# Order of TensorE's work in a fused attention and mixing kernel: low parts last, the first turn inside an angle product, value products at the end of a half unit

## The chip, the cores and the metric

The kernel runs on one core of a Trainium2 chip. The metric is device time in microseconds (us): the median of three runs before the change is 1183.68 (1183.5 to 1184.48). The engines are named as the profile names them: PE is TensorE (its weight loads are PEld), DVE is VectorE, ACT is ScalarE, POOL is GpSimd, SP issues most DMAs.

## The reference

Eight batches of eight heads, 576 positions, head width 64. Attention keeps only scores within `tau` of a row's maximum; its output, with the heads side by side (512 wide), goes through a mixing block with sines and cosines of an angle.

```python
scores = scale * np.matmul(q, k.transpose(0, 1, 3, 2))
thresh = np.max(scores, axis=-1, keepdims=True) - tau
scores = np.where(scores >= thresh, scores, -1000000000.0)
attn = np.exp(scores - max); attn = attn / (sum + 1e-09)
x = np.matmul(attn, v)                       # heads side by side
theta = x @ w_theta
zr = x * np.cos(theta); zi = x * np.sin(theta)
y = w_tok_r @ zr + w_tok_i @ zi              # over positions, per batch
u = x + y
out = u + np.maximum(u @ w_ch, 0.0)
```

The two lines with `max` and `sum` are shortened; everything else is as the reference has it.

## The kernel before, in words

Everything on PE is in an order written out by the program; the other engines' orders come from a scheduler that goes by priorities and by a timeline of its own. PE's order is the order in which the code issues its instructions.

**Attention.** The outer loop goes over *half units* t: for each of 32 pairs of heads nine of them (four blocks of 128 queries for each of two heads, and one for the 64 queries left of both). A half unit issues, in this order: the scores of half unit t+3 (`begin`, L264, tile s_ps, one such tile in all), a piece of mixing work (`fill`), the turning round of half unit t's weights (`flip` and `flip_last`, L312 and L327, tiles t_ps), what is due at t (`todo`), and a second piece of mixing work (`fill`). Due are: the value products (`values`, L347, tile o_ps, 20 matmuls in fp32, 256 or 320 columns), the scaling of a pair's result (`normalize`, L363 to L372), at the end of a batch the splitting of its result into parts (`split_x`), and one half unit later the start of the batch's mixing.

DVE reads a score tile and frees it (L268), ACT takes the exponential (L285), DVE applies the threshold (L286), ACT copies turned weights out (L317, L319, L330, L334) and value products (L348).

**Mixing** (`moe`) is a generator that hands out its PE work in pieces with a price; each `fill` takes pieces for about 820 units of price. For exactness every factor is split into a high and a low part of reduced precision (fp32r), so that a product is three terms: high by high and two mixed ones. The four blocks of 128 columns are numbered 0 to 3; `ORDER` lists the steps:

- a0 to a3: the angles (`angle`, `product`, L381, tile th_ps): 24 matmuls each, 12 for each half h of the positions. ACT moves them out (L416); DVE reduces them to one turn (L420, L421).
- s01 and s23: sines and cosines of two blocks (`sines`): DVE takes the magnitude (L430), ACT loads the table with sine (L434), computes two cosines and two sines (L438, L439) and loads the table with the exponential again (L443); POOL multiplies by x (L450; DVE in the last batch). ACT's group has a priority far above the rest.
- f0 to f3: turning round of z (`flip`, L462, tile z_ps), whose results ACT and DVE split into zh and zl (L464, L465). "t0f1" means: f1 in three pieces between the pieces of t0.
- t0 to t3: the products over positions (`token`, L478 to L480, tile y_ps): 27 matmuls for each half; DVE adds them to x (L482), then u is split (`split_u`, L104, L100, L109).
- last the channel products (L381, tile c_ps), again 24 matmuls for each block, and the output (L523, L527).

All PSUM tiles but s_ps share six buffers of one tag (`ps_t`). The z tiles have three buffers. The tiles in which q and k are loaded share four buffers (`temp`) with the angles.

Low parts: xl comes from POOL for blocks 0 and 1 and from DVE for 2 and 3; zl from DVE; ul from POOL for blocks 0 to 2, and from DVE for block 3, whose uh comes from ACT.

Of the kernel before, what the change touches and what calls it, by code (L numbers as in the profile page):

```python
# [10 lines left out]
F32 = mybir.dt.float32  # L11
# [20 lines left out]
ATTENTION, SINES = 20, 10000  # L32
# [3 lines left out]
ORDER = "a0 a1 s01 a2 a3 f0 s23 t0f1 t1f2 t2f3 t3"  # L36
# [3 lines left out]
def tile_attn_moe(  # L40
# [11 lines left out]
    nc = tc.nc  # L52
    B, NP, D, _, S = qT.shape
    P = 128
    DM = 512
    NM = DM // P
    HS = S // 2
    SP = S + 64
    NK = 9
# [315 lines left out]
    def product(ps, wm, parts, hs, outer=False):  # L375

        terms = [(a, bb, c) for a, bb in ((0, 0), (0, 1), (1, 0)) for c in range(NM)]
        if outer:
            terms.sort(key=lambda x: x[2])
        for n, (a, bb, c) in enumerate(terms):  # L380
            nc.tensor.matmul(ps[:, :HS], wm[:, a, c, :], parts[c][bb][:, hs], start=(n == 0), stop=(n == 11))  # L381
            if n % 4 == 3 and n < 11:
                yield 524
# [6 lines left out]
    parts = {}  # L390
# [8 lines left out]
    def moe(b):  # L399
        last = b == B - 1  # L400
# [7 lines left out]
        def angle(m):  # L408
            th = temp("th")
            wm = get_wm(0, m)  # L410
            for h in range(2):
                hs = slice(h * HS, (h + 1) * HS)
                ps = ps_t.tile([P, 512], F32, tag="t", name="th_ps")
                yield from product(ps, wm, xs, hs, outer=(m == 0 and h == 0))

                nc.scalar.activation(out=th[:, hs], in_=ps[:, :HS], func=AF.Copy, scale=1.0 / TURN)  # L416
                yield 524
# [52 lines left out]
        def token(m):  # L470
            zz = zs.pop((m, "T"))
            x = xT[b * NP + m]
            for h in range(2):
                hs = slice(h * HS, (h + 1) * HS)
                ps = ps_t.tile([P, 512], F32, tag="t", name="y_ps")
                for c in range(NK):
                    zh, zl = zz[c]
                    nc.tensor.matmul(ps[:, :HS], zh, wt_h[:, c, hs], start=(c == 0), stop=False)  # L478
                    nc.tensor.matmul(ps[:, :HS], zh, wt_l[:, c, hs], start=False, stop=False)  # L479
                    nc.tensor.matmul(ps[:, :HS], zl, wt_h[:, c, hs], start=False, stop=(c == NK - 1))  # L480
                    yield 393
# [11 lines left out]
        for what in ORDER.split():  # L493
# [3 lines left out]
            if what == "a":  # L497
                yield from angle(m)
# [17 lines left out]
        for m in range(NM):  # L516
            wm = get_wm(1, m)
            u = xT[b * NP + m]
            for h in range(2):
                hs = slice(h * HS, (h + 1) * HS)  # L520
                ps = ps_t.tile([P, 512], F32, tag="t", name="c_ps")
                yield from product(ps, wm, us, hs, outer=last or (m == 0 and h == 0))
# [3 lines left out]
                yield 524  # L526
# [45 lines left out]
    with tc.manual_schedule(engines={nc.tensor.engine}):  # L572
# [3 lines left out]
        for t, (n, i, j) in enumerate(halfs):  # L576
# [5 lines left out]
            with tc.high_priority(offset=ATTENTION):  # L582
# [5 lines left out]
                for fn, a in todo.pop(t, ()):  # L588
                    fn(*a)
# [7 lines left out]
            fill()  # L597
            if n + 1 < B * NP:
# [60 lines left out]
```

## Time and profile before

| what | value |
|---|---|
| median of three runs | 1183.68 us |
| profiled execution | 1179.78 us, span 1178.0 us |
| PE busy | 1049.4 us (89%) |
| DVE, ACT, POOL busy | 853.2, 748.9, 381.9 us |
| mean granted PE clock | 0.956 of full speed |

The profiled execution is 3.9 us below the median of the three runs; 1.8 us of it lie outside the span. Busy PE is time in which a matmul is under way, and matmuls overlap, so the waits of PE and the stretches in which its granted clock is below one say more than its busy share.

### The profile page before, as it was taken

To read this page: it belongs to the slowest core of one execution; us is meant where nothing else is said; L and a number is where in the kernel's file an instruction comes from. 1 tells how busy PE (TensorE), PEld (TensorE's weight loads), DVE (VectorE), ACT (ScalarE), POOL (GpSimd) and SP (SyncE) were. 2 spreads that over 40 slices of the span, in tenths; PEclk is the share of its full clock that TensorE was granted. 3 is DMA by queue.
4 is the path that set the end of the run, shared out by engine and by line. 5 is a ranking of instruction groups with operands and counts; after the bars stand their busy time and mean duration, and the time that the engine had idled before them with its cause. 6 is when DMAs were issued, how large, how long until landed. Compare 5 with 4: busy or idle time off the path is not lost.

```text
span 1178.0 us, 20979 instructions
## 1 busy us (share of the span) xinstructions
PE 1049.4 (89%) x7648; PEld 923.3 (78%) x7648; DVE 853.2 (72%) x2111; ACT 748.9 (64%) x1411; POOL 381.9 (32%) x295
## 2 busy tenths in 40 slices
PE   3756688999979999899989998899989999799998
PEld 2544577899869888798878987798878988699798
DVE  7999987676767767776777667776776767677462
ACT  5656677765686666865686657765687656765350
POOL 2011323531353233432344324522335313531110
PEclk9776799999989999999999999999989999899999
DMA  8623523213331152212432142311532143300421
GB/s 259 185 90 90 159 57 103 57 49 107 103 102 55 32 162 77 78 51 62 140 104 72 32 134 83 99 51 54 148 95 65 46 116 103 88 21 1 117 68 58
DMA packets 55175, 105.24 MB, mean 89 GB/s; under 512 B 11936, under 2 KB 20128, under 8 KB 55072
## 3 DMA queue, kind: packets, MB, share of 16 engines
q1 hardware_dynamic: 45856, 70.35, 20.4%
q0 software_dynamic: 9216, 33.56, 9.8%
q8 instruction: 60, 0.98, 0.3%
q14 instruction: 43, 0.35, 0.1%
HBM read 90.24 MB, written 13.63 MB: 88 GB/s over the span
## 4 chain that ended last, share of the span: by engine, by line
PE 66%; DVE 13%; ACT 9%; DMA 4%; issue 3%; POOL 2%; SPq 1%; ACTq 0%; POOLq 0%; DVEq 0%
PE o_ps L347 12%; PE s_ps L264 11%; PE t_ps L312 8%; PE y_ps L478 6%; PE y_ps L480 6%; PE c_ps L381 6%; PE y_ps L479 6%; PE th_ps L381 6%; DMA qraw<-in_qT_dram 4%; DVE sc L268 3%; DVE s_sb L286 3%; PE z_ps L462 2%; POOL xl L109 2%; ACT s_sb L285 1%; ACT z L438 1%
## 5 line engine op out<-in xcount | busy, mean ns | idle before, releaser
L268 DVE TENSOR_SCALAR_CACHE_REDUCE sc<-s_ps 128x576 f32<-128x576 f32 x288 | 217.5, 755 | 129.3 <-PE s_ps L264 125.3
L286 DVE SCALAR_TENSOR_TENSOR s_sb<-sc,nm,s_sb 128x576 f32<-128x576 f32 x288 | 258.3, 901 | 55.6 <-ACT s_sb L285 53.0
L285 ACT ACTIVATE s_sb<-sc,nm 128x576 f32<-128x576 f32 x288 | 223.4, 778 | 114.3 <-DVE sc L268 113.6
L264 PE MATMUL s_ps<-k,qq 128*128 128x288 f32 (+1 forms) x1344 | 240.0, 308 | 59.4 <-DVE sc L268 48.8
L264 PEld LDWEIGHTS s_ps<-k,qq 128*128 128x128 f32 x1344 | 202.8, 199 | 72.5 <-DVE sc L268 45.7
L347 PE MATMUL o_ps<-a,v 128*64 128x320 f32 (+1 forms) x1280 | 183.7, 433 | 20.0 <-ACT a L319 19.2
L478 PE MATMUL y_ps<-wt_h,zh 128*128 128x288 f32 x576 | 188.5, 327 | 6.7 <-DVE xT L482 5.9
L312 PE MATMUL t_ps<-ident,s_sb 128*128 128x128 f32 x1152 | 185.2, 286 | 6.3 <-ACT xT L348 4.9
L480 PE MATMUL y_ps<-wt_h,zl 128*128 128x288 f32 x576 | 172.0, 299 | 11.3 <-DVE zl L465 11.3
L479 PE MATMUL y_ps<-wt_l,zh 128*128 128x288 f32 x576 | 170.9, 297 | 0.0
L317 ACT COPY a<-t_ps 128x512 f32<-128x512 f32 x256 | 148.1, 578 | 32.1 <-PE t_ps L312 31.5
L347 PEld LDWEIGHTS o_ps<-a,v 128*64 128x64 f32 x1280 | 91.6, 144 | 91.5 <-ACT a L319 22.4
L312 PEld LDWEIGHTS t_ps<-ident,s_sb 128*128 128x128 f32 x1152 | 148.7, 147 | 9.3 <-ACT xT L348 5.8
L109 POOL TENSOR_TENSOR k<-kraw,k 128x576 fp32r<-128x576 f32 x62 | 91.9, 1483 | 197.2 <-ACT k L100 196.5
L214 POOL TENSOR_TENSOR qq<-qraw,qq 64x576 fp32r<-64x576 f32 x62 | 98.5, 1589 | 124.9 <-ACT qq L212 86.7
L178 POOL DMA_DIRECT2D wm<-wm_dram x64 | 37.0, 579 | 279.0 <-PE c_ps L381 170.9
L478 PEld LDWEIGHTS y_ps<-wt_h,zh 128*128 128x128 f32 x576 | 109.8, 191 | 14.0 <-DVE xT L482 7.5
L480 PEld LDWEIGHTS y_ps<-wt_h,zl 128*128 128x128 f32 x576 | 109.3, 190 | 13.3 <-DVE zl L465 13.3
L479 PEld LDWEIGHTS y_ps<-wt_l,zh 128*128 128x128 f32 x576 | 110.2, 191 | 0.0
L450 POOL TENSOR_TENSOR z<-z,xT 128x576 f32<-128x576 f32 x56 | 83.8, 1516 | 46.3 <-issue 32.3
L381 PE MATMUL c_ps<-uh,wm 128*128 128x288 f32 x512 | 97.6, 303 | 0.1
L381 PE MATMUL th_ps<-xh,wm 128*128 128x288 f32 x512 | 89.0, 300 | 0.4 <-ACT xh L100 0.4
(77 smaller groups left out, 1547.2 us busy)
## 6 DMA issues: line engine op xcount, KB each, us to landing
wm<-wm_dram POOLq DMA_DIRECT2D x64, 512.0 KB, 4.2
qraw<-in_qT_dram SPq DMA_DIRECT2D x128, 144.0 KB, 3.0
kraw<-in_kT_dram SPq DMA_DIRECT2D x128, 144.0 KB, 2.9
out_dram<-xT SPq DMA_DIRECT2D x32, 288.0 KB, 4.1
v<-in_vp_dram SPq DMA_DIRECT2D x32, 256.0 KB, 2.8
wraw<-in_w_tok_dram SPq DMA_DIRECT2D x9, 576.0 KB, 4.0
wraw<-in_w_theta_dram SPq DMA_DIRECT2D x4, 512.0 KB, 5.0
wm_dram<-whi SPq DMA_DIRECT2D x8, 256.0 KB, 2.3
```

The costliest lines, as they stand in the source:

```text
L109: eng_lo.tensor_tensor(out=lo, in0=src, in1=hi.bitcast(F32), op=ALU.subtract)
L264: nc.tensor.matmul(ps[:, h, d0:d1], st, kk, start=(x == 0), stop=(x == len(todo) - 1))
L268: nc.vector.tensor_scalar(out=sc.rearrange("p (a b) -> p a b", a=2), in0=ps[:, :, :HS], scalar1=-1.0, scalar2=None, op0=ALU.mult, op1=ALU.min,
L285: nc.scalar.activation(out=e, in_=u.ps[j], func=AF.Exp, bias=nm[:, j : j + 1], scale=-1.0)
L286: nc.vector.scalar_tensor_tensor(out=e, in0=u.ps[j], scalar=nm[:, 2 + j : 3 + j], in1=e, op0=ALU.is_le, op1=ALU.mult, accum_out=u.pr.rows[ ...
L312: nc.tensor.transpose(out=tp[:, c * P : (c + 1) * P], in_=u.sf[:, k0 + c * P : k0 + (c + 1) * P], identity=ident)
L317: nc.scalar.copy(out=t.a[:, :, j, q0 : q0 + P], in_=tp.rearrange("p (c q) -> p c q", c=4))
L347: nc.tensor.matmul(o[64 * j : 64 * j + 64, :w], st, mv, start=(c == 0), stop=(c == 4))
L381: nc.tensor.matmul(ps[:, :HS], wm[:, a, c, :], parts[c][bb][:, hs], start=(n == 0), stop=(n == 11))
L478: nc.tensor.matmul(ps[:, :HS], zh, wt_h[:, c, hs], start=(c == 0), stop=False)
L479: nc.tensor.matmul(ps[:, :HS], zh, wt_l[:, c, hs], start=False, stop=False)
L480: nc.tensor.matmul(ps[:, :HS], zl, wt_h[:, c, hs], start=False, stop=(c == NK - 1))
```

## The change

Three things are reordered on PE, and with them the pools' and the scheduler's choices on the other engines.

1. `product` runs high by high, then low weights by high x, then high weights by low x (before: the mixed term with low x came second). For the first block of angles and of channels it now runs the two high terms of both halves before the terms with low parts of either (`together`), with two PSUM tiles open; before, the first half alone was sorted by input block. In `token` all products with zh come first and those with zl last.
2. f0 is no longer a step by itself: its three pieces go between the last pieces of a3 ("a3f0").
3. What is due at t (`todo`) is issued after the second `fill` of the half unit, no longer ahead of it.

```diff
-ORDER = "a0 a1 s01 a2 a3 f0 s23 t0f1 t1f2 t2f3 t3"
+ORDER = "a0 a1 s01 a2 a3f0 s23 t0f1 t1f2 t2f3 t3"
...
-        terms = [(a, bb, c) for a, bb in ((0, 0), (0, 1), (1, 0)) for c in range(NM)]
-        if outer:
-            terms.sort(key=lambda x: x[2])
...
+        work = [[(h, a, bb, c) for a, bb in ((0, 0), (1, 0), (0, 1)) for c in range(NM)] for h in range(2)]
+        if together:
+            runs = [work[0][:8], work[1][:8], work[0][8:], work[1][8:]]
+        else:
+            runs = work
+        tiles, count = {}, [0, 0]
+        for run in runs:
+            for n, (h, a, bb, c) in enumerate(run):
+                hs = slice(h * HS, (h + 1) * HS)
+                if h not in tiles:
+                    tiles[h] = ps_t.tile([P, 512], F32, tag="t", name="m_ps")
+                nc.tensor.matmul(
+                    tiles[h][:, :HS], wm[:, a, c, :], parts[c][bb][:, hs], start=(count[h] == 0), stop=(count[h] == 11)
+                )
+                count[h] += 1
+                if count[h] == 12:
+                    todo(tiles[h], hs)
+                if n % 4 == 3:
+                    yield 524
...
-                for c in range(NK):
-                    zh, zl = zz[c]
-                    nc.tensor.matmul(ps[:, :HS], zh, wt_h[:, c, hs], start=(c == 0), stop=False)
-                    nc.tensor.matmul(ps[:, :HS], zh, wt_l[:, c, hs], start=False, stop=False)
-                    nc.tensor.matmul(ps[:, :HS], zl, wt_h[:, c, hs], start=False, stop=(c == NK - 1))
-                    yield 393
+                work = [(zz[c][0], w[:, c, hs]) for c in range(NK) for w in (wt_h, wt_l)]
+                work += [(zz[c][1], wt_h[:, c, hs]) for c in range(NK)]
+                for n, (z, w) in enumerate(work):
+                    nc.tensor.matmul(ps[:, :HS], z, w, start=(n == 0), stop=(n == len(work) - 1))
+                    if n % 3 == 2:
+                        yield 393
...
             if what == "a":
-                yield from angle(m)
+                other = flip(ms[1]) if turns else iter(())
+                for n, cost in enumerate(angle(m)):
+                    yield cost
+                    if n > 1:
+                        yield next(other, 0)
+                for cost in other:
+                    yield cost
...
-                for fn, a in todo.pop(t, ()):
-                    fn(*a)
...
             fill()
+            with tc.high_priority(offset=ATTENTION):
+                for fn, a in todo.pop(t, ()):
+                    fn(*a)
```

**What stands where.** PE, at the start of the mixing of a batch in the middle of the program (a0). The tile named th_ps or m_ps takes the angles, xh and xl are the parts of x, wm is the weights. Before:

```order
L312 MATMUL t_ps<-ident,s_sb 128x128 x4
L381 MATMUL th_ps<-xh,wm_6474 128x288
L381 MATMUL th_ps<-xl,wm_6474 128x288
L381 MATMUL th_ps<-xh,wm_6474 128x288 x2
L381 MATMUL th_ps<-xl,wm_6474 128x288
L381 MATMUL th_ps<-xh,wm_6474 128x288 x2
L381 MATMUL th_ps<-xl,wm_6474 128x288
...
L381 MATMUL th_ps<-xh,wm_6474 128x288 x2
L381 MATMUL th_ps<-xl,wm_6474 128x288
L381 MATMUL th_ps<-xh,wm_6474 128x288 x5
```

And the same place in the changed kernel (its line L388 is the matmul of `product`):

```order
L388 MATMUL m_ps<-xh,wm_6500 128x288 x8
L312 MATMUL t_ps<-ident,s_sb 128x128 x4
L327 MATMUL t_ps<-ident,s_sb 128x128
L388 MATMUL m_ps<-xh,wm_6500 128x288 x8
...
L388 MATMUL m_ps<-xl,wm_6500 128x288 x4
L312 MATMUL t_ps<-ident,s_sb 128x128 x4
L388 MATMUL m_ps<-xl,wm_6500 128x288 x4
```

The first use of xl has moved from the second matmul of the mixing to the seventeenth, with scores and turns between.

PE again, in the same batch at a3, around the value product of the last quarter (o_ps from a_6560, 64x320). Before:

```order
L381 MATMUL th_ps<-xh,wm_6737 128x288 x4
L312 MATMUL t_ps<-ident,s_sb 128x128 x4
L347 MATMUL o_ps<-a_6560,v_6344 64x320 x8
L347 MATMUL o_ps<-a_6561,v_89 64x320 x2
L363 MATMUL rb_ps<-ident,rb 128x128 x4
...
L381 MATMUL th_ps<-xl,wm_6737 128x288 x4
L381 MATMUL th_ps<-xh,wm_6737 128x288 x4
...
L462 MATMUL z_ps<-ident,z 128x128 x5
```

In the changed kernel (L473 is the turn of z):

```order
L388 MATMUL m_ps<-xl,wm_6748 128x288 x4
L312 MATMUL t_ps<-ident,s_sb 128x128 x4
L473 MATMUL z_ps<-ident,z 128x128 x4
L388 MATMUL m_ps<-xh,wm_6748 128x288 x4
L347 MATMUL o_ps<-a_6544,v_6332 64x320 x8
L347 MATMUL o_ps<-a_6545,v_89 64x320 x2
L363 MATMUL rb_ps<-ident,rb 128x128 x4
...
L473 MATMUL z_ps<-ident,z 128x128
L388 MATMUL m_ps<-xh,wm_6748 128x288 x4
```

The first four turns of z0 now stand ahead of the value product, and the other pieces between pieces of a3.

ACT, in the same batch, at the second group of sines (s23: z from th). Before, with two table loads:

```order
L285 ACTIVATE s_sb<-sc,nm 128x576
L464 CAST zh<-z_ps 128x512
L434 ACT_TABLE_LOAD
L438 ACTIVATE z<-z,small 128x576
L439 ACTIVATE z<-th 128x576 x2
L212 CAST qq_83<-qraw_6828 128x576
L438 ACTIVATE z<-z,small 128x576
L443 ACT_TABLE_LOAD
```

In the changed kernel (L449 is the cosine, L450 the sine, L285 the exponential of the attention):

```order
L475 CAST zh<-z_ps 128x512
L445 ACT_TABLE_LOAD
L449 ACTIVATE z<-z,small 128x576
L450 ACTIVATE z<-th 128x576 x2
L317 COPY a_6778<-t_ps 128x4x128
L330 COPY a_6779<-t_ps 128x128
L285 ACT_TABLE_LOAD
L285 ACTIVATE s_sb<-sc,nm 128x576
L449 ACT_TABLE_LOAD
L449 ACTIVATE z<-z,small 128x576
L454 ACT_TABLE_LOAD
```

An exponential has come in between the third and the fourth of the sines, with a table load for it and one more for the cosine behind it; it is so in seven of the eight batches.

## Rows read from the trace of the kernel before

**Rows 1.** The page, busy time of each engine with share and instructions

```profile
PE 1049.4 (89%) x7648; PEld 923.3 (78%) x7648; DVE 853.2 (72%) x2111; ACT 748.9 (64%) x1411; POOL 381.9 (32%) x295
```

**Rows 2.** Waits of PE, whole span: us in total, times, longest

```profile
PE o_ps L347 <- ACT a L319: 19.2, 10, 2.6
PE th_ps L381 <- POOL xl L109: 13.9, 14, 1.6
PE y_ps L480 <- DVE zl L465: 11.3, 8, 1.7
...
PE c_ps L381 <- DVE ul L109: 5.9, 8, 0.8
PE y_ps L478 <- DVE xT L482: 5.9, 7, 0.8
```

**Rows 3.** Waits of PE from 60 to 200 us

```profile
PE s_ps L264 <- DVE sc L268: 33.8, 21, 5.6
```

**Rows 4.** Busy time by stretch (start:end, length, engines, granted clock PEclk), seven sine stretches

```profile
190.00:230.00 40.00, 34.13 (x248) 29.11 (x247) 29.65 (x67) 32.01 (x59) 21.20 (x15) 0.96 0.28 79
325.00:365.00 40.00, 33.48 (x235) 29.15 (x234) 27.83 (x65) 30.33 (x56) 20.03 (x14) 0.91 0.27 78
462.00:495.00 33.00, 26.47 (x196) 22.04 (x196) 25.32 (x55) 26.24 (x49) 18.43 (x13) 1.00 0.31 93
596.00:625.00 29.00, 22.98 (x158) 17.88 (x157) 21.19 (x42) 22.93 (x41) 17.47 (x12) 0.94 0.32 89
732.00:760.00 28.00, 21.89 (x161) 17.44 (x159) 21.31 (x43) 22.89 (x41) 16.48 (x12) 1.00 0.32 93
865.00:900.00 35.00, 29.80 (x204) 24.89 (x203) 25.16 (x56) 27.33 (x51) 18.92 (x14) 0.90 0.30 90
1000.00:1030.00 30.00, 23.50 (x155) 19.30 (x155) 19.18 (x42) 23.31 (x42) 16.67 (x12) 0.89 0.33 96
sum 235.00, PE 192.25 PEld 159.80 DVE 169.65 ACT 185.04 POOL 129.20; mean PE 27.46 PEld 22.83 DVE 24.24 ACT 26.43 POOL 18.46
```

**Rows 5.** Chain of waits from 600 to 760 us: start, length, what

```profile
637.54 2.84 PE o_ps L347 x20
...
712.15 1.06 PE th_ps L381 x8
713.22 0.44 PE t_ps L312 x4
```

**Rows 6.** Timeline of PE at the value product: start, us, [idle before]

```profile
599.88 4.60 PE L347 MATMUL o_ps<-a,v 128*64 128x320 f32 x20 [2.57 <-ACT a L319]
```

**Rows 7.** Timeline of ACT, both sine groups of that batch

```profile
593.75 1.28 ACT L434 ACT_TABLE_LOAD   x1
595.05 0.78 ACT L438 ACTIVATE z<-z,small 128x576 f32<-128x576 f32 x1
...
604.54 0.78 ACT L211 ACTIVATE qraw<-qraw,small 128x576 f32<-128x576 f32 x1 [2.01 <-DMA qraw<-in_qT_dram]
...
611.31 1.28 ACT L434 ACT_TABLE_LOAD   x1
```

**Rows 8.** Timeline of POOL, then of PE, behind the second sine group

```profile
621.04 1.93 POOL L109 TENSOR_TENSOR k<-kraw,k 128x576 fp32r<-128x576 f32 x1
...
627.59 0.69 PE L264 MATMUL s_ps<-k,qq 128*128 128x288 f32 x4
```

**Rows 9.** Timeline of DVE, the same operation without and beside POOL's work

```profile
590.73 0.46 DVE L420 TENSOR_SCALAR km<-th 128x576 f32<-128x576 f32 x1 [0.34 <-issue]
...
597.30 1.71 DVE L420 TENSOR_SCALAR km<-th 128x576 f32<-128x576 f32 x1
```

**Rows 10.** Timeline of DVE, then of ACT, between t3 and the channel products

```profile
542.85 0.46 DVE L482 TENSOR_TENSOR xT<-y_ps,xT 128x288 f32<-128x288 f32 x1 [0.63 <-PE y_ps L480]
...
543.35 0.68 ACT L100 CAST uh<-xT 128x576 fp32r<-128x576 f32 x1
```

**Rows 11.** Waits of PE from 1040 us to the end

```profile
PE th_ps L381 <- POOL xl L109: 2.2, 2, 1.6
```

More of the change, by code (lines that the diff above doesn't have):

```diff
@@ L372, in normalize, with product @@
             nc.vector.tensor_tensor(out=x[r, 512:S], in0=x[r, 512:S], in1=tl[r, 64 * j : 64 * j + 64], op=ALU.mult)
-    def product(ps, wm, parts, hs, outer=False):
-        terms = [(a, bb, c) for a, bb in ((0, 0), (0, 1), (1, 0)) for c in range(NM)]
-        if outer:
-            terms.sort(key=lambda x: x[2])
[L380 to L383, printed above, removed]
+    def product(wm, parts, todo, together):
+        work = [[(h, a, bb, c) for a, bb in ((0, 0), (1, 0), (0, 1)) for c in range(NM)] for h in range(2)]
[17 more added lines that the diff above has]
+                    yield 524
     def halves(which):
@@ L410, in angle, with evict @@
             wm = get_wm(0, m)
[L411 to L414, printed above, removed]
+            def evict(ps, hs):
                 nc.scalar.activation(out=th[:, hs], in_=ps[:, :HS], func=AF.Copy, scale=1.0 / TURN)
-                yield 524
+            yield from product(wm, xs, evict, m == 0)
             km = temp("km")
@@ L518, in moe, with evict @@
             u = xT[b * NP + m]
[L519 to L522, printed above, removed]
+            def evict(ps, hs):
                 nc.vector.scalar_tensor_tensor(
@@ L525, in moe @@
                 )
-                yield 524
+            yield from product(wm, us, evict, m == 0)
             nc.sync.dma_start(outT[b, m * P : (m + 1) * P, :], u)
```

## The prediction

> **What bounds the kernel now.** I began with the page's busy times: PE leads, and ACT and DVE have a quarter to a third of the span to spare [rows 1]. Then the waits of PE, sorted by whom it waits for [rows 2], then the same by stretch. The score waits on DVE lie in the first 200 us, 33.8 of them from 60 to 200 [rows 3]; there DVE is late with the weights' preparation, and nothing of the change touches that. From 190 us on PE works through its list almost without a gap, and each batch, 135 us long by the starts of the stretches (190 to 1000 in six) [rows 4], loses time in one place: the sine stretch, in which ACT serves two groups of sines. The seven such stretches with attention beside them hold 235 us, of which PE is busy 192.25: it idles 42.75, or 6.1 in each [rows 4]. In five of the seven the granted clock is 0.89 to 0.96, so that a part of them ran at 1.2 instead of 2.4 GHz; length times what lacks to 1 is 1.6 + 3.6 + 1.7 + 3.5 + 3.3 = 13.7 us. How this looks: the value product of 20 matmuls takes 2.84 us elsewhere [rows 5] and 4.60 right behind an idle 2.57 [rows 6].
>
> What the waits cost depends on PE alone, as it is the engine whose list is full: a wait that goes is time won until another operand is late. So the working is: which wait goes, and what is late next.
>
> **Low x last.** The first angle product of a batch waits for xl from POOL, 13.9 us in all, 2.2 of them in the tail [rows 2, 11]; so 11.7 beside attention. xl is now wanted sixteen matmuls later, 2.1 us at 1.06 for eight [rows 5], with a score and a turn between. The longest single wait is 1.6 [rows 2] and the two of a batch sum to about 2. I count −11.7; if POOL's list delays xl as much as it is moved, 0, which I see no reason for, since the mixing starts behind `split_x` by the same two half units as before.
>
> **Low u last.** The waits for ul are 5.9 in eight places [rows 2]. What is late next is uh of block 3: before, sorted by block, it was wanted by the tenth matmul, now by the fourth. DVE adds the last y at 542.85, ACT's uh is ready at 543.35 + 0.68 = 544.03 [rows 10], 1.2 after, or 1.4 after PE's last y. Until the fourth matmul PE has a turn (0.44), its small companion and three matmuls (0.4), 1.05 in all. So 0.33 stays in each of eight, 2.6: −3.3. Bounds: −5.9 if the cast is early, +2 if ACT serves the turn's copies first.
>
> **Low z last.** The waits for zl, 11.3 [rows 2], go altogether at their place: zl is wanted after eighteen matmuls, not at the third. But they lie in the sine stretch, and there ACT's list decides, so I count the stretch as a whole.
>
> **The sine stretch.** I laid PE's and ACT's new lists beside each other, with durations from the rows.
>
> First group. ACT loads a table at 593.75 [rows 7] and serves nobody until its group is done; PE has used up its work 3.6 later and waits 2.57, to 599.88, for the copy L319 [rows 6]. In the new list the group has the same length, but PE has more to do: four turns of z0 (0.44) and a quarter of a3 stand ahead of the value product, and the group begins about 1 us earlier against PE, as the score ahead of it does. The quarter needs a PSUM tile that ACT frees after the group; for that I get a wait of 0.6. The z turns themselves find their operand ready: a load of 1.28, a cosine of 0.78 [rows 7] and a product on POOL, at most the 1.93 of the like k operation [rows 8], make 4.0 after the group's start, and PE comes at 4.4.
>
> Behind it DVE is late. Beside POOL's four products DVE's km takes 1.71 instead of 0.46 [rows 9], and so do its neighbours; so far that fell into PE's long wait. Now the second turn and the next piece of z0 come 1.2 earlier than DVE frees their tiles: 1.2.
>
> Second group. Here the list of ACT speaks against the change. z3's magnitude reaches ACT late, so the scheduler put an exponential among the sines: two table loads more at 1.28 and one exponential, 0.78 like the cosine of the same shape [rows 7], 3.3 us in each of seven batches, 18 us of loads in all. Also the second eviction of a2 stands behind the first group now, so DVE finishes that angle about 2 later, its buffer takes the next q later, and ACT, which waits for q's landing already (L211) [rows 7], waits longer. The last cosine comes about 5 later than before. Behind it on POOL stand z3's two products and the key part k2 of the next pair; k2 begins at 621.04 and takes 1.93 now, and its score runs at 627.59 [rows 8]: 4.6 of slack. With 5 lost on ACT and some 2 won on PE the slack is gone: a wait of 1.75 of the score for POOL, and 0.7 of the value product before it. The first matmul of y's second half waits 0.75 for DVE as it does now (5.9 in seven [rows 2]).
>
> Sum: 0.6 + 1.2 + 1.75 + 0.7 + 0.75 = 5.0 instead of 6.1, −1.1 × 7 = −7.7. Bounds: with the late cosine fully paid, 8 (+13); with only 0.6 and 0.75 left, 1.4 (−33).
>
> The Trainium skill has a rule against just this: "ScalarE: Activation LUTs", Rules for kernel authors, says to do all of one table set before switching, and its section What ACT_TABLE_LOAD costs puts a switch at a load of 1.283 us and a drain of 1.38. This trace agrees with the load, not with the drain: the activation behind the load of 593.75 starts at 595.05 [rows 7]. By that rule the group would be held another 2.8 in each batch.
>
> **The clock.** The dips come with the long waits of the stretch. Shorter ones, more spread, should leave some of it out; two of seven stretches show no dip though they idle as long, 6.5 and 6.1 [rows 4], so it is not certain either way. I take half of 13.7: −6.9; bounds 0 and −13.7.
>
> **Value products at the end.** They are moved past one piece of mixing, and so is the start of each batch's mixing, since both hang on the same list of due steps. Against each other they stand as before, so I count nothing; matmul kinds change as often as before. The output DMA and the weights' DMA on POOL hang on mixing's place and move with it. One piece (0.7 us) moves from the start, where PE idles, to the tail: +0.7, against about 1 won there on the 2.2 for xl [rows 11]. I count 0 for the tail, bounds −4 and +3.
>
> **Sum.** −11.7 − 3.3 − 7.7 − 6.9 = −29.6 us. The profiled execution has 1179.78 us, 3.9 below the median of 1183.68; −29.6 from the median gives 1154.
>
> **The rivals.**
>
> *All of it goes.* The sine stretch keeps only 0.6 + 0.75: −33; with −11.7, −3.3 and the whole clock −13.7, that is −62: 1122. For it: none of the engines is above three quarters. Against it: two table loads more, and POOL's list behind the cosine. 0.13.
>
> *The split sine group eats the stretch's gain.* Idle stays at 6.1 and the clock where it is: −11.7 − 3.3 = −15, 1169. For it: ACT is busy 185 of 235 us in these stretches [rows 4], and everything that PE needs there goes through it. 0.18.
>
> *A switch of tables costs more than its load.* If ACT also empties first, by another 1.4 for each of two, the score behind waits 2.8 more, 20 in all: −29.6 + 20 gives 1174. Against it: 0.02 between a load's end and what follows [rows 7]. 0.05. This is the drain of the page of the Trainium skill named above.
>
> *Slower.* The held ACT leaves PE without free PSUM tiles, so that the whole hold is idle time: 3.3 for loads and exponential and 3 for the late q, 6.3 more in each of seven, +44, less the 15 of x and u: +29, 1213. It turns to slower from 2.1 us a batch above today's 6.1. For it: six tiles serve turns, y, z and value products, and PE's list runs dry in today's first group after 3.6 us. Against it: in the new list ACT serves two copies between the sines, and the second group has long y pieces beside it, which need no new tile. 0.08.
>
> *Nothing.* The gains and the new waits cancel. 0.04.
>
> **How the numbers follow.** The forecast has 0.52, and its own range is 1140 to 1166 by the clock's and the second group's bounds. The range that holds eight in ten takes in the 1169 and 1174 above and half of the way to 1122: 1128 to 1177. A difference of 0.2% (2.4 us) is about what a measurement of this kernel can tell from none. Faster by more: 0.52 + 0.13 + 0.18 + 0.05 = 0.88, less 0.01 for forecasts that just miss: 0.87; within: 0.05; slower: 0.08.
>
> **What would show it.** In the waits of PE the rows on xl, zl and ul are gone or below 1 us in all; on uh from ACT some 2 to 3 us appear. The value product's wait for L319 falls from 2.57 to below 1 each. New rows: a score waiting for POOL's k, seven times about 1.75, and turns waiting for DVE. ACT has fourteen table loads more, at 1.28. In the seven sine stretches PE idles about 5, and the clock's sum falls below 13.7. Batches follow each other by about 131 us instead of 135. It is wrong if the stretches idle more than 7 us each, if the clock dips where it did not, or if waits for DVE appear outside them.

## The result, and the profile after

The changed kernel takes 1169.9 us (median of four runs) against 1184.08; the ratio is 0.988 (95% 0.9854 to 0.9905): 14.2 us faster where 29.6 were forecast. One of the four, at a mean granted clock of 0.834, took 1224.78 and is left out of the ratio; the others took 1167.96 to 1170.49. The profiled execution has a span of 1168.7 against 1178.0, and all that follows on waits is about these 9.3 us, since the profiled execution of the kernel before was 3.9 below its median. By the starts of value products 0.4 of them were lost up to the tenth, 4.7 won in the six batches from the tenth to the 58th (194.51 to 999.86, so 134.23 each instead of 135.02), and 5.0 won behind that. The forecast had 131 for a batch.

The page's busy line: PE has the same instructions and is busy less, ACT has fourteen instructions more and 16 us.

```profile
PE 1042.9 (89%) x7648; PEld 916.8 (78%) x7648; DVE 838.1 (72%) x2111; ACT 765.0 (65%) x1425; POOL 368.6 (32%) x295
```

The sine stretches by windows, against [rows 4]: the granted clock is 1.00 in all seven, and PE idles 235 - 202.62 = 32.4 us, 4.6 in each, instead of 6.1.

```profile
190.00:230.00 40.00, 35.62 (x264) 30.92 (x264) 29.06 (x71) 36.52 (x66) 20.93 (x15) 1.00 0.30 87
...
593.00:622.00 29.00, 24.58 (x181) 20.32 (x179) 18.23 (x44) 25.30 (x44) 16.30 (x12) 1.00 0.33 98
...
996.00:1026.00 30.00, 26.09 (x192) 21.63 (x191) 19.47 (x46) 27.23 (x48) 17.64 (x13) 1.00 0.32 95
sum 235.00, PE 202.62 PEld 170.43 DVE 158.22 ACT 208.72 POOL 126.06; mean PE 28.95 PEld 24.35 DVE 22.60 ACT 29.82 POOL 18.01
```

The waits of PE over the span, against [rows 2]: L319, xl, zl and ul are gone from the places that they had, and nine others stand between the tenth and the 58th value product. The first of them misleads: of its 62.1 us 12.9 lie behind 190 us, the rest at the start, where the kernel before has 48.8, too.

```profile
PE s_ps L264 <- DVE sc L268: 62.1, 43, 6.0
PE m_ps L388 <- ACT uh L100: 11.9, 8, 1.6
PE m_ps L388 <- ACT th L426: 8.6, 7, 1.4
...
PE z_ps L473 <- DVE zl L476: 5.5, 7, 0.8
PE t_ps L312 <- DVE zl L476: 5.0, 6, 1.3
PE s_ps L264 <- DVE rows L352: 4.9, 7, 0.7
PE o_ps L347 <- DVE xT L493: 3.5, 7, 0.5
PE s_ps L264 <- POOL k L109: 3.4, 7, 0.5
PE s_ps L264 <- DVE rows L353: 3.1, 6, 1.6
```

So a batch still waits 8.66 us where it waited 8.83; both are the listed waits of PE between the tenth and the 58th value product, divided by six. What the batch has beside them fell from 126.19 to 125.57. The new waits have three sources.

First, the second sine group. On ACT's timeline an exponential stands among the sines, with a table load on either side, as the prediction read from the order:

```profile
612.47 1.24 ACT L450 ACTIVATE z<-th 128x576 f32<-128x576 f32 x2
...
614.37 1.28 ACT L285 ACT_TABLE_LOAD   x1
615.66 0.78 ACT L285 ACTIVATE s_sb<-sc,nm 128x576 f32<-128x576 f32 x1
616.45 1.28 ACT L449 ACT_TABLE_LOAD   x1
617.75 0.78 ACT L449 ACTIVATE z<-z,small 128x576 f32<-128x576 f32 x1
618.54 1.28 ACT L454 ACT_TABLE_LOAD   x1
```

Second, the start of a batch. PE no longer waits for xl, but the next score waits for DVE, which has an xl operation ahead of the sc that frees the one score tile (timeline of DVE, then of PE):

```profile
570.72 1.39 DVE L109 TENSOR_TENSOR xl<-xT,xh 128x576 fp32r<-128x576 f32 x1
572.03 0.75 DVE L268 TENSOR_SCALAR_CACHE_REDUCE sc<-s_ps 128x576 f32<-128x576 f32 x1
...
572.85 0.81 PE L264 MATMUL s_ps<-k,qq 128*128 128x288 f32 x4 [1.58 <-DVE sc L268]
```

Third, the start of the channel products. The last y is added at 675.28, 0.46 long; ACT then has a turn's copies and an exponential ahead of the cast uh, which PE wants at the fourth matmul (timeline of ACT, then of PE):

```profile
675.43 0.58 ACT L317 COPY a<-t_ps 128x512 f32<-128x512 f32 x1 [1.19 <-PE t_ps L312]
675.91 0.27 ACT L330 COPY a<-t_ps 128x128 f32<-128x128 f32 x1
676.07 0.79 ACT L285 ACTIVATE s_sb<-sc,nm 128x576 f32<-128x576 f32 x1
676.75 0.67 ACT L100 CAST uh<-xT 128x576 fp32r<-128x576 f32 x1
...
677.47 1.46 PE L388 MATMUL m_ps<-uh,wm 128*128 128x288 f32 x9 [1.57 <-ACT uh L100]
```

### The profile page after: what moved, and what is told of

Same layout as the page of the kernel before. It is cut to its first block, busy times and chain, and to the rows that moved or that the text cites. A ratio compares the mean times of both kernels' runs of the same rounds, so it can differ in the third digit from the quotient of the medians.

```text
span 1168.7 us, 20962 instructions
## 1 busy us (share of the span) xinstructions
PE 1042.9 (89%) x7648; PEld 916.8 (78%) x7648; DVE 838.1 (72%) x2111; ACT 765.0 (65%) x1425; POOL 368.6 (32%) x295
## 4 chain that ended last, share of the span: by engine, by line
PE 56%; DVE 19%; ACT 17%; issue 4%; DMA 3%; SPq 0%; ACTq 0%; DVEq 0%
PE y_ps L490 14%; PE m_ps L388 12%; PE s_ps L264 10%; PE o_ps L347 10%; PE t_ps L312 6%; DVE sc L268 5%; DVE s_sb L286 4%; DMA qraw<-in_qT_dram 2%; ACT s_sb L285 2%; ACT z L449 2%; ACT L445 2%; ACT L454 2%; ACT z L450 1%; ACT a L317 1%; PE z_ps L473 1%
## 5 line engine op out<-in xcount | busy, mean ns | idle before, releaser
L286 DVE SCALAR_TENSOR_TENSOR s_sb<-sc,nm,s_sb 128x576 f32<-128x576 f32 x288 | 273.2, 949 | 108.8 <-ACT s_sb L285 104.5
L264 PE MATMUL s_ps<-k,qq 128*128 128x288 f32 (+1 forms) x1344 | 250.6, 315 | 85.8 <-DVE sc L268 62.1
L264 PEld LDWEIGHTS s_ps<-k,qq 128*128 128x128 f32 x1344 | 200.5, 199 | 120.1 <-DVE sc L268 67.9
L285 ACT ACTIVATE s_sb<-sc,nm 128x576 f32<-128x576 f32 x288 | 223.6, 779 | 102.3 <-DVE sc L268 101.7
L347 PE MATMUL o_ps<-a,v 128*64 128x320 f32 (+1 forms) x1280 | 176.0, 422 | 3.5 <-DVE xT L493 3.5
L490 PE MATMUL y_ps<-wt_h,zh 128*128 128x288 f32 x576 | 165.2, 305 | 0.5 <-ACT zh L475 0.4
L490 PE MATMUL y_ps<-wt_l,zh 128*128 128x288 f32 x576 | 162.9, 301 | 0.0
L347 PEld LDWEIGHTS o_ps<-a,v 128*64 128x64 f32 x1280 | 91.1, 141 | 67.9 <-issue 12.1
L490 PE MATMUL y_ps<-wt_h,zl 128*128 128x288 f32 x576 | 102.9, 304 | 0.0
L388 PE MATMUL m_ps<-xh,wm 128*128 128x288 f32 x512 | 90.1, 305 | 9.0 <-ACT th L426 8.6
L388 PE MATMUL m_ps<-uh,wm 128*128 128x288 f32 x512 | 85.0, 301 | 11.9 <-ACT uh L100 11.9
L461 POOL TENSOR_TENSOR z<-z,xT 128x576 f32<-128x576 f32 x56 | 79.2, 1440 | 25.1 <-ACT z L449 15.4
L109 POOL TENSOR_TENSOR ul<-xT,uh 128x576 fp32r<-128x576 f32 x24 | 34.3, 1427 | 163.4 <-DVE uh L104 107.5
```

Source lines behind the costliest of these rows:

```text
L109: eng_lo.tensor_tensor(out=lo, in0=src, in1=hi.bitcast(F32), op=ALU.subtract)
L264: nc.tensor.matmul(ps[:, h, d0:d1], st, kk, start=(x == 0), stop=(x == len(todo) - 1))
L285: nc.scalar.activation(out=e, in_=u.ps[j], func=AF.Exp, bias=nm[:, j : j + 1], scale=-1.0)
L286: nc.vector.scalar_tensor_tensor(out=e, in0=u.ps[j], scalar=nm[:, 2 + j : 3 + j], in1=e, op0=ALU.is_le, op1=ALU.mult, accum_out=u.pr.rows[ ...
L347: nc.tensor.matmul(o[64 * j : 64 * j + 64, :w], st, mv, start=(c == 0), stop=(c == 4))
L388: nc.tensor.matmul(tiles[h][:, :HS], wm[:, a, c, :], parts[c][bb][:, hs], start=(count[h] == 0), stop=(count[h] == 11))
```

## The experiments

All ratios are to the kernel before, measured together with each, with 95% intervals of about 0.0025 either way (3 us, so some 4 for a difference of two); kernels measured at different times are compared by ratio, times 1183. "Batch" and "waits" are worked out as above from each kernel's profiled execution, in us for one batch.

| kernel | median | ratio | interval | batch | waits |
|---|---|---|---|---|---|
| before | 1184.08 | 1 | | 135.02 | 8.83 |
| changed kernel | 1169.9 | 0.988 | 0.9854 to 0.9905 | 134.23 | 8.66 |
| u_v: values at their old place | 1153.6 | 0.9756 | 0.973 to 0.9781 | 132.18 | 6.67 |
| u_f0: z0 turned behind a3 | 1172.47 | 0.9913 | 0.989 to 0.9936 | 134.77 | 9.06 |
| v_f0: both undone | 1191.68 | 1.0072 | 1.0045 to 1.0099 | 137.12 | 9.47 |
| whole: no exponential in the group | 1157.04 | 0.9773 | 0.9748 to 0.9797 | 132.05 | 6.97 |
| u_x: x in the old order | 1173.72 | 0.9931 | 0.9905 to 0.9957 | 134.53 | 8.62 |
| u_u: u in the old order | 1173.95 | 0.9922 | 0.99 to 0.9944 | 134.46 | 8.21 |
| v_z: u_v, z in the old order | 1154.61 | 0.9762 | 0.9747 to 0.9776 | 131.81 | 6.45 |
| v_xl: u_v, xl behind the score | 1143.33 | 0.9656 | 0.9632 to 0.968 | 130.53 | 5.24 |
| v_u: u_v, block 3 of u last | 1148.98 | 0.9702 | 0.9678 to 0.9726 | 131.72 | 6.26 |
| v_xlu: u_v with both of these | 1137.55 | 0.9621 | 0.9605 to 0.9636 | 129.64 | 4.71 |
| after_fix: changed kernel with three mends | 1135.39 | 0.9615 | 0.9586 to 0.9643 | 129.82 | 5.16 |
| xu_alone: before, x and u low last | 1204.03 | 1.0185 | 1.0164 to 1.0206 | 138.78 | 10.56 |
| x_alone | 1202.56 | 1.0188 | 1.0161 to 1.0216 | 138.72 | 10.65 |
| u_alone | 1205.4 | 1.0213 | 1.0184 to 1.0242 | 138.86 | 10.41 |
| xu_t5: xu_alone, fifth buffer, no exponential in the group | 1160.37 | 0.9811 | 0.9784 to 0.9839 | 132.39 | 6.53 |
| before_t5: before, the same two edits | 1185.4 | 1.0012 | 0.9992 to 1.0031 | 136.39 | 8.85 |
| b_dve: v_xlu, last copy on DVE | 1133.27 | 0.9586 | 0.9573 to 0.9599 | 129.00 | 3.63 |
| best_t5: b_dve, fifth buffer | 1119.76 | 0.9462 | 0.9436 to 0.9488 | 126.70 | 2.50 |

**Where the values stand, and the turn of z0.** u_v takes the value products back ahead of the second piece of mixing:

```
                     del units[n, i]
+                for fn, a in todo.pop(t, ()):
+                    fn(*a)
...
-            with tc.high_priority(offset=ATTENTION):
-                for fn, a in todo.pop(t, ()):
-                    fn(*a)
```

> The changed kernel with one part undone: the value products and the other due steps stand again ahead of the half unit's second piece of mixing. In this order ACT's second sine group is whole again (33 table loads as before the change, against 47). Theory A (the split group is what eats the sine stretch's gain, and it comes from this part, which I had costed at nothing): ACT is free about 3.3 us earlier in each of seven stretches, the waits behind the split group (z_ps for zl 0.8, score for rows 0.7 and 0.5, score for POOL's k 0.5, value product for xT 0.5, with some 0.2 of refill each) go in good part: 2 to 3.5 us a batch, 15 to 24 us in all, so 1146 to 1155 us. Theory B (ACT's list in the stretch is full with or without two loads, the waits only change name): within 4 us of the changed kernel, 1166 to 1174.

u_f0 undoes one word, v_f0 this and the values:

```
-ORDER = "a0 a1 s01 a2 a3f0 s23 t0f1 t1f2 t2f3 t3"
+ORDER = "a0 a1 s01 a2 a3 f0 s23 t0f1 t1f2 t2f3 t3"
```

> The changed kernel with one part undone: the first z is turned by itself behind the last angle product, as before. Theory A (the gain of the change is the clock, and this part is what keeps it, since it fills the long wait of the first sine group): the value product waits 2 us or more again, the granted clock falls in some of the stretches as before the change (about 13 us), 1178 to 1186 us. Theory B (the clock stays with the other parts, too): the clock stays at 1.00 from 190 us on, and the time is within 4 us of the changed kernel's 1170.

> Low parts last alone, with the value products at their old place and the first z turned by itself behind the last angle product (the fourth corner beside the kernels with either or both). Theory A (the two edits act against each other: only with both does an exponential fall between the sines, so turning z0 within the last angle is worth far more without the values at the end): 12 to 20 us slower than the kernel that has the turn but not the values at the end, 1166 to 1174 us, with clock below 1.00 in some sine stretches. Theory B (the parts add up): the turn is worth the 2.6 us that it was worth beside values at the end, 1155 to 1158 us.

The part that I had costed at nothing costs 14.7 us (0.988 against 0.9756). u_f0 has the clock of its theory A with the time of theory B; v_f0 is 18 us slower than even its theory A had. With the values at the old place the early turn of z0 looks worth 37 us (1.0072 to 0.9756), beside values at the end not surely anything (0.9913 to 0.988). But most of the 37 is not the turn's: v_f0 is one of the kernels in which a load of q starts late (below). For the like pair with low z in its old order, 50 us (xu_alone 1.0185, v_z 0.9762), a fifth buffer, with the exponentials kept out of the group, gives 44 back without the turn (xu_t5 0.9811). So it is not shown that the two edits act against each other in time beyond the table loads: only with both does an exponential fall between the sines; the traces of u_v, u_f0 and v_f0 have 33 table loads, that of the changed kernel 47. The clock follows the turn: behind the seventh slice of the page (some 200 us) all twelve kernels with the early turn have a 9 throughout, and each of the eight without it falls to 8 somewhere. The row on the page (40 slices, in tenths) is shown first for u_v, then for u_f0, where y waits up to 3.9 us for zh.

```profile
PEclk9876799999999999999999999999999999999999
```

```profile
PEclk9776789899999999999989999999999999999999
```

whole takes the exponential out of the group and leaves the values at the end; PE's and POOL's lists are the same word for word.

```
+        act = nc.scalar.activation(out=e, in_=u.ps[j], func=AF.Exp, ...
+        for x in held:
+            after(act, x)
...
+            if ms[0] == 2:
+                held[:] = [exp]
```

> The changed kernel with one order added: exponentials that are issued behind the second sine group of a batch may not run before its last cosine. PE's and POOL's lists stay as they are word for word; on ACT fourteen table loads go and seven exponentials move one place back. Theory A (the two extra loads in each of seven stretches are what the changed kernel lost): the second group ends 2.6 us earlier for what stands behind it, the waits for rows, POOL's k, zl (z_ps) and xT, 2.5 us a batch with their refill, go for the most part: 1150 to 1158 us. Theory B (the loads are cheap, and what costs is that the value products come a piece later): the waits change name, 1164 to 1171 us.

It is 12.7 us faster than the changed kernel (0.988 to 0.9773): theory A. Fourteen loads of 1.28 are 18 us, 23 with the seven exponentials that ACT served inside the groups, so a bit over half of the hold reached the end.

**Low x, low u and low z in the new order.** u_x and u_u put the old order of terms back in one of the two products, v_z in the token product of u_v:

```
+            terms = [(a, bb, c) for a, bb in ((0, 0), (0, 1), (1, 0)) for c in range(NM)]
+            if every or (first and h == 0):
+                terms.sort(key=lambda x: x[2])
```

> The changed kernel with one part undone: the angle product takes its terms in the old order (low x before low w, and sorted by block in the first half of the first angle). By the prediction's term 11.7 us come back: 1180 to 1183. By theory A (the score behind DVE's xl operations at each batch's start takes the place of the wait for xl, 1.9 against 2.3 us from start to start in each of six): the xl waits of 2 us a batch return, the score's wait of 1.58 goes, and the time moves by 1 to 4 us: 1170 to 1174.

> The changed kernel with one part undone: the channel product takes its terms in the old order (sorted by block in the first half). By the prediction's term 3.3 us come back: 1173. By theory A (uh of block 3 stands behind the turn's copies and an exponential on ACT, so that what was 0.7 to 0.8 for ul became 1.57 for uh): the wait for uh (11.9) goes, that for ul (5.9) returns, and the kernel gets 5 to 7 us faster: 1163 to 1165.

> Values at their old place, x and u low parts last, z0 turned inside the last angle, but the token product in its old order (zh, zh, zl of each block together). Theory A (with z0 turned early, zl is wanted at the third matmul of y, while DVE still has ACT's late casts before it: 1.6 a batch as before): 8 to 12 us slower than 1153.6, so 1161 to 1166. Theory B (the old order is no worse, since the new one wants all of a z's blocks by the eighteenth matmul and so meets ACT's sine group earlier, which is what makes low parts last alone slower, 1191.7): 1150 to 1156.

x is worth some 6 us, u some 5, both with intervals that touch that of the changed kernel. u_x has the time of its theory A, but not its way: with x in the old order the score at a batch's start waits 1.58 just the same, and between the tenth and the 58th value product PE never waits for xl (u_x: POOL, then PE).

```profile
570.92 3.31 POOL L109 TENSOR_TENSOR xl<-xT,xh 128x576 fp32r<-128x576 f32 x2 [2.97 <-PE m_ps L388]
...
573.69 0.81 PE L264 MATMUL s_ps<-k,qq 128*128 128x288 f32 x4 [1.58 <-DVE sc L268]
...
574.47 0.29 PE L406 MATMUL m_ps<-xl,wm 128*128 128x288 f32 x1
```

With values at the end PE waits for the score first, whatever the order of x, and POOL's xl is done by then (570.92 + 3.31). The order is worth 0.30 a batch there; behind the 58th value product it is worth 3.2, where two waits for xl come back.

My theory on u fell: undone, 5.5 of the wait for uh stay and 4.4 for ul come back, so the old order was no way out. z makes no difference where z0 is turned early (0.9762 against 0.9756); where it is not, low z last is worth 13 us (v_f0 1.0072 against xu_alone 1.0185, which differ in nothing else).

v_xl and v_u mend what x and u ran into, at u_v:

```
+            if c == NM - 1 and b < B - 1:
+                copy(eng, hi, xT[b * NP + c])
+                lows.append((hi, lo, xT[b * NP + c]))
...
+        for hi, lo, src in lows:
+            after(nc.vector.tensor_tensor(out=lo, in0=src, in1=hi.bitcast(F32), op=ALU.subtract), negated)
```

```
+                runs = [[x for x in w if x[3] != late] for w in work] + [[x for x in w if x[3] == late] for w in work]
...
+            yield from product(wm, us, evict, m == 0, NM - 1)
```

> Values at their old place, and DVE's xl of the last block put behind the next score's sc; nothing else differs on any engine but km and nm changing places once a batch. Theory A (the score at each batch's start waits 1.60 us only because two xl operations of 1.4 us stand before its sc on DVE): that wait falls to 0.3 or less in seven batches, 8 to 13 us off, 1141 to 1146 us. Theory B (xl is then late for the angle product, or the following score waits instead): within 3 us of 1153.6.

> Values at their old place, and in the first channel product of a batch all terms of block 3 last (nine matmuls of both halves before the first of block 3, twelve at the end). Theory A (what is left of the u wait is the cast of block 3 alone, wanted at the fourth matmul): the wait for uh, 3.2 in all, goes, some 0.2 of refill with each of eight, 1149 to 1151 us. Theory B (DVE's ul of block 3 or the eviction of the first half is late instead): within 1 us of 1153.6 or slower.

v_xl is 11.8 us faster than u_v (0.9756 to 0.9656), by one operation of DVE in another place, and the wait for sc falls from 3.26 to 1.72 a batch. v_u wins 6.4 (within some 4), where its wait held 3.2. Together:

> The two edits together that are each faster than values at their old place alone: DVE's xl of the last block behind the next score's sc (10.3 off), and block 3 last in the first channel product (4.6 off). They lie at two ends of a batch, so I expect them to add: 1153.6 - 10.3 - 4.6 = 1138.7, within 1136 to 1142. If both only move PE into the next wait, 1143 as the first alone.

after_fix puts the three mends (whole, xl behind the score, block 3 last) into the changed kernel:

> The changed kernel, values at the end and all, with three edits: no exponential inside the second sine group, DVE's xl of the last block behind the next score's sc, block 3 last in the first channel product. If the shortfall of the changed kernel lies in these three places (12.9 for the split group as measured, 1.6 a batch for the score behind xl, 1.57 a batch for uh, each with some 0.2 of refill, in seven or eight batches): 1169.9 - 12.9 - 11 - 13 = 1133, within 1129 to 1140. If they are only names for one pace that ACT sets, no more than one of them can be won: 1150 to 1157.

It is 31 us faster than the changed kernel (0.988 to 0.9615), twice the shortfall, so that lay in no pace of ACT's that no mend could pass. But two of the three places gave it. whole has 12.7; the 18.7 beyond it came with block 3 last, where the wait for uh had held 11.9. The order of xl moved nothing in the six batches: in the changed kernel DVE has one xl ahead of the sc and one behind it already, and in after_fix the score waits as before (DVE, then PE):

```profile
555.04 1.39 DVE L109 TENSOR_TENSOR xl<-xT,xh 128x576 fp32r<-128x576 f32 x1
556.35 0.74 DVE L270 TENSOR_SCALAR_CACHE_REDUCE sc<-s_ps 128x576 f32<-128x576 f32 x1
...
557.16 0.80 PE L266 MATMUL s_ps<-k,qq 128*128 128x288 f32 x4 [1.58 <-DVE sc L270]
```

That the time came out as expected, with 11 us counted for this place, is luck.

**Low parts last by themselves.** xu_alone is the kernel before with only the new order in the angle and channel products; x_alone and u_alone have it in one.

> The kernel before with low x and low u last and nothing else (token order, turn of z0 and value products as before). By the prediction's terms, 11.7 for x and 3.3 for u, 15 us off: 1169. Theory A (the waits for xl give way to the score that stands behind two xl operations on DVE, 1.6 against 1.9 a batch; ul gives way to uh, 0.4 against 0.75): x is worth 2 to 4, u 3: 5 to 7 us off, 1177 to 1180 us.

> The kernel before with low x last in the angle product and nothing else. By the prediction's term 11.7 us off: 1171 to 1173. Theory A (what is won ahead of the sine stretch is waited for inside it, where ACT's list sets the pace, and a turn that comes earlier against ACT's second group waits 2 to 3 us for a PSUM tile, with the clock down): slower than before, 1186 to 1200, with z_ps waiting for ACT's copies and a granted clock below 0.956 over the span. Theory B (u is the one that does the harm): 1178 to 1183.

> The kernel before with low u last in the channel product and nothing else. By the prediction's term 3.3 us off: 1180. Theory A (x does the harm in the stretch): 1178 to 1183. Theory B (u does it): 1190 to 1204.

All three are 22 to 25 us slower than the kernel before. For x_alone theory A had the sign and the wait, for u_alone theory B; that either does it alone, and both together no more, was in no theory of mine, and the prediction is off by 36 for the two. What holds them stands in the timeline of u_alone (SP, POOL, ACT and PE):

```profile
610.37 1.11 SPq L199 DMA_DIRECT2D qraw<-in_qT_dram  x2
...
615.37 1.42 POOL L214 TENSOR_TENSOR qq<-qraw,qq 64x576 fp32r<-64x576 f32 x1 [3.88 <-ACT qq L212]
616.74 0.59 POOL L178 DMA_DIRECT2D wm<-wm_dram  x1
...
616.82 1.11 SPq L199 DMA_DIRECT2D qraw<-in_qT_dram  x2
...
623.56 0.77 ACT L211 ACTIVATE qraw<-qraw,small 128x576 f32<-128x576 f32 x1 [6.21 <-DMA qraw<-in_qT_dram]
624.24 0.57 ACT L317 COPY a<-t_ps 128x512 f32<-128x512 f32 x1
...
624.95 1.09 PE L488 MATMUL z_ps<-ident,z 128*128 128x128 f32 x4 [3.97 <-ACT a L317]
```

Read from below: PE's turn of z waits 3.97 for a PSUM tile that ACT's copy frees, and goes on at about half the clock (1.09 for four, 0.60 elsewhere). The copy stands behind ACT's work on the second head's q, which waits 6.21 for its load. SP started that load 6.4 us after the first head's, when POOL's qq had freed the first one's buffer (615.37 + 1.42), and just as POOL's weights set out.

In the kernel before, the second load starts 4.1 us after the first, 2.4 ahead of the weights, and ACT waits 0.71 for it (SP, POOL, ACT):

```profile
601.04 1.11 SPq L199 DMA_DIRECT2D qraw<-in_qT_dram  x2
...
605.14 1.11 SPq L199 DMA_DIRECT2D qraw<-in_qT_dram  x2
...
607.52 0.67 POOL L178 DMA_DIRECT2D wm<-wm_dram  x1
...
608.73 0.78 ACT L211 ACTIVATE qraw<-qraw,small 128x576 f32<-128x576 f32 x1 [0.71 <-DMA qraw<-in_qT_dram]
```

x_alone, xu_alone and v_f0 have the gap of 6.4 to 6.5; u_v, u_f0 and the changed kernel have 2.4. q, k, th and km share four buffers of one size, and which one q gets hangs on the order of the others. xu_t5 gives a fifth and keeps exponentials out of the second sine group by the edit of whole; before_t5, with both edits, is its control. The edit of the buffers:

```
-        return pool.tile([P, S], dt, tag="t576", name=name, bufs=4)
+        return pool.tile([P, S], dt, tag="t576", name=name, bufs=5)
```

> Low x and low u last alone (the kernel that took 1204.0), with a fifth buffer for the tiles that q, k, th and km share, and no exponential inside the second sine group (else the scheduler would put one there now). PE's list is word for word that of the kernel of 1204.0. Theory A (that kernel is slow because the load of q's second head waits for the buffer that q's first head frees on POOL, starts 6.4 us after the first instead of 2.4 to 4.1, meets the weights' transfer, and holds ACT's list up to 6 us): the two loads start within 3 us of each other, ACT's waits for q fall from 58 us to 30 or less, and the 21 us go, 1165 to 1183. Theory B (PE merely reaches the stretch too early for ACT's sines, whatever q does): 1195 to 1206.

> The control: the kernel before with the same two edits (fifth buffer, no exponential inside the second sine group). Theory A: its second q was not held by the first, so it gains little: 1172 to 1184. If a fifth buffer helps whatever the order, it gains as much as low x and u last alone do by it, 1160 or less.

With the same list on PE, 1.0185 becomes 0.9811, 44 us, more than expected, and the control stays at 1.0012. The waits of ACT for q, of xu_alone and of xu_t5:

```profile
ACT qraw L211 <- DMA qraw<-in_qT_dram: 58.2, 24, 6.0
```

```profile
ACT qraw L212 <- DMA qraw<-in_qT_dram: 19.8, 17, 1.9
```

The loads start 3.9 us apart now, not within 3 as expected, and the second 6.6 earlier against the value product. So low x and low u last are worth 24 us against the control, and with four buffers all of it and more was lost. The two edits also changed places on the lists of ACT, DVE and POOL, so the late load is not tried quite by itself; 38 us of ACT's waits for q went with it. That the meeting with the weights, beside the late start, makes the load longer (6.7 from issue to ACT's start, 3.6 in the kernel before) was not tried by itself.

**A faster version.** b_dve is v_xlu with the copy of a pair's last turn on DVE (`nc.vector.tensor_copy` at L319), best_t5 has the fifth buffer too.

> The same two edits, and the copy of a pair's last turn (L319, 128x512) on DVE instead of ACT. Theory A (the value product's wait for L319, 2.3 a batch, lasts only because the copy stands behind a table load of 1.28 on ACT, while DVE waits there for ACT): 1 to 2 us a batch, 8 to 14 us off 1138.7, so 1125 to 1131. Theory B (DVE is slowed there by POOL's products, km 1.71 instead of 0.46, and its score work is then late): 1136 to 1145.

> The fastest kernel so far (1133.3: values at their old place, DVE's xl behind the score, block 3 last in the first channel product, the last turn's copy on DVE) with a fifth buffer for q, k, th and km. ACT still waits 23 us for q in all there, with PE's wait for POOL's z (1.0 a batch) ahead of it rather than behind: theory A, q is late for ACT but not for PE, 1130 to 1135; theory B, an earlier q lets ACT turn z earlier, 1122 to 1130.

b_dve is 4 us faster than v_xlu, half of the least that I expected: L319 is gone, but turns wait for zl and xT instead, 1.0 a batch. best_t5 takes 1119.76, 0.9462 of the kernel before and a little below its theory B, the fastest here.

## Why the prediction was wrong

Its sign was right and the time lies in its range; the size was twice too large. Its own steps follow, each with what it foresaw for a batch, and what the profiled execution has:

- **Value products at the end, 0.** This step failed: "against each other they stand as before, so I count nothing". They move the mixing by one piece against the turns, and with z0's early turn the scheduler's own timeline then puts an exponential among the sines. I had seen the split in the order and put it down to z0's turn and z3's late magnitude alone. The step costs 14.7 us over the kernel (u_v); the split taken out by itself gives 12.7 back (whole).
- **Low x last, -1.67.** xl went from the list as said, 1.94 a batch; in its place, and not in the working, stands the score behind xl on DVE, 1.58. Net -0.36. But with values at the end both are so in the old order of x, too (u_x): the step took the start of the mixing, against the scores, as unmoved. At u_v the score's wait could be won, by 11.8 us, with DVE's order (v_xl); in the changed kernel it is still open (after_fix). It is one of the signs that the prediction had named against itself, a wait for DVE outside the stretches.
- **Low u last, -0.47.** I had 0.33 left, as it is in u_v (0.33). With values at the end it is 1.57: ACT serves the turn's copies first, the bound that I had named. Net +0.78; this, too, is the values' place and not the order of u, which undone costs 5 us (u_u).
- **The sine stretch, -1.1.** The other listed waits, nearly all there, fell from 6.11 to 5.50 a batch (the windows, which count the idle time of fixed stretches, have 6.1 and 4.6). The value product's wait is gone; of the new ones the quarter of a3 waits 1.23 for ACT's th (0.6 foreseen), the score 0.48 for POOL's k (1.75 foreseen), and turns and scores take the rest.
- **The clock, half of 13.7 us.** All dips went, not half. But what a batch has beside its listed waits fell by only 0.62, 4.3 us in seven. Why not more is open: by the pages the matmuls of the value products (L347) are busy 176.0 instead of 183.7 us, but those of the scores (L264) 250.6 instead of 240.0.
- **The tail, 0.** 5.0 were won behind the 58th value product. The seventh sine stretch lies there as well, so this is not the tail alone; 3.2 of it go with x in the old order (u_x).

-0.36 + 0.78 - 0.61 - 0.62 = -0.81, against the measured -0.79. The sum must come out, as it only divides up one measured time; the first step has no term in it, its cost lies in the wait for uh and in the stretch. The rival "the split sine group eats the stretch's gain" had the time, 1169, and the right culprit, but not its way: x and u did not bring 15, and the clock did not stay.

The rule of the Trainium skill that I weighed, to do all of one table set before switching ("ScalarE: Activation LUTs", Rules for kernel authors), holds here: 12.7 us for seven split groups. Its drain of 1.38 on top of a load does not show: the exponential starts 0.01 behind the end of its load (614.37 + 1.28, 615.66), and the next load 0.01 behind the exponential's (615.66 + 0.78, 616.45).

That u_v comes out at my forecast is in part luck: there, too, the score waits 1.6 at a batch's start, where x should have won 1.67, and a tail that won 7 makes up for it.

## What to carry to other kernels

Where one engine's list is full, an edit's price is not the wait that it removes but the next thing on the same engines' lists; ask of each helper (DVE behind xl, ACT ahead of uh) what stands before it now. Where a scheduler decides the other engines' order, price an edit only together with the others: values at the end and an early turn, neither of which did it alone, together put a table switch into a group. And before a change of order is judged, look whether a load got another buffer of a shared pool: one buffer more, with the exponentials kept out of the sine group, turned a loss of 22 us into a gain of 22, while the kernel before gained nothing by both. Look also, after a mend, whether the wait that it was meant for is gone; a total that comes out as expected does not show it.

## What the runs showed of the hardware

- The clock. After a wait of 2.57 us the granted clock was 0.63 over a value product, which took 4.60 instead of 2.84 [rows 5, 6]; after one of 3.97 it was 0.50, the lower of its two levels, over four turns in u_alone, 1.09 instead of 0.60. In the changed kernel, whose longest wait behind 190 us is 1.6, it stayed at 1.00, though as much time was waited in all.
- DVE's subtraction of two SBUF tiles takes 1.39 while POOL does the same on its two blocks, and 0.75 with POOL idle (ul at 677.63 in the changed kernel). The Trainium skill's "GPSIMD Engine Reference", Specifications, has the two engines share their SBUF interfaces and contend when DVE has two SBUF inputs; the trace agrees as far as the longer time goes.
- The load of one head's q, two of 144 KB, took 6.7 us from its issue to ACT's start on it beside the weights' 512 KB, and 3.6 with 2.4 us of start on them.
